# Attention, then a Fourier mix and a feed-forward layer, on one core: transform parts moved behind the next scores, and one row's copies made once and brought in by DMA

## The chip, the core and the metric

The kernel runs on one core of a Trainium2 chip. The core has a matrix engine (PE; its weight loads are shown apart as PEld), a vector engine (DVE), an activation engine (ACT), a general engine (POOL) and a queue engine (SP) that issues most of the transfers. Each engine takes its own instructions in order and waits on semaphores for the others. The metric is the device time of one execution in microseconds.

## What is computed

Attention over 4 batches, 8 heads, 768 tokens of head size 64: each token sees the 4 first tokens and the 128 up to itself. Its output, with heads side by side, is `x` of 4 x 768 x 512. Then a two-dimensional Fourier transform of each batch is added, and a normalized feed-forward layer on top:

```python
keep = is_sink | in_window
scores = np.where(keep, scale * q @ k.T, -1e9)
x = softmax(scores) @ v
u = x + real(fft(fft(x, axis=1), axis=2))
un = (u - mean(u)) / sqrt(var(u) + 1e-6)
out = u + relu(un @ w_ch1) @ w_ch2
```

## The kernel before

**Attention** runs in 96 steps. A step `s` is block `g = s // 4` of 128 query tokens (24 blocks, six to a batch) and a pair of heads `k = s % 4`. The work on one pair is spread over later steps by a table of lags: scores on PE at once (`scores`), a merge and a masked maximum on DVE one step later (`merge`, `soft1`), the exponential on ACT after two (`expo`), the transposes of a pair of pairs after three (`trans_p`, PE), copies and masks on ACT and POOL, and attention times values after seven (`av`, PE). Per block come a transpose of the sink columns (`trans_sink`, seven steps after the block's first, PE, tile `pk`), the turn back to tokens (`turn_x`, tile `x`) and the scaled store into `u` (`store_x`, DVE). Because the lags of `trans_p`, `av` and `turn_x` fall on even steps, an odd step gives PE nothing but its scores, `trans_sink` (where `k` is 3) and transform work.

A step issues its loads on SP first, then the scores, then what the lists in `SCHEDULE` name for ACT, DVE, POOL and PE, in their order. From step 97 on (`CUT`) the order on an engine is left to the scheduler of the framework. The scores have two PSUM buffers of two banks each, so the scores of step `s + 1` need `soft1` of step `s - 1` to be done.

**The transform** of batch b is created when its fourth block is stored (steps 25, 49, 73 and 97) and put into the same steps as events. First the blocks are folded (`fold_n`, `fold_m`, on DVE and POOL; `fold_hi` on ACT, `fold_lo` on DVE): tiles `f`, `gh`, `gl`. Fifteen steps after its creation `stage1` starts: five products `za0`, `za1`, `zr`, `zb0`, `zb1`, each in two parts, one for a step; then `stage2a` and `stage2b` (`dc`, `a`, `b`). Each result lies in one PSUM bank, is copied by ACT (`z_hi`, `a_copy`) and finished by DVE (`z_lo`, `combine`), and then the next product takes a bank: tag `fft`, or for a product begun at a step with `k` of 2 (`X_AT`) the bank `x`, which `turn_x` uses too.

**The first token's row.** Token 0 has no place in the six blocks. Its attention output for all batches is made on DVE in steps 10 to 20 and stored into `x0_dram` (`first_row`). Per batch, `load_row` brings it in on 33 partitions (tile `xr`), `put_row` copies it to row 0 of block 3 of `u` once the folds have read that row, `mid_sum` folds it, `mid_hi` copies it rounded into `sph` and `mid_row` puts what the rounding left into partition 32 of `sph`. The last matmul of `za0`, `za1` and `zr` reads `sph`. All of these are DVE's, except that in the last batch `mid_hi` is ACT's; `ROW` holds their steps after the creation.

**The feed-forward layer** begins on PE when attention ends and runs alone from about 283 us on.

Of the kernel before, what the change touches and what calls it, by code (L numbers as in the profile page):

```python
# [11 lines left out]
F32 = mybir.dt.float32  # L12
F32R = mybir.dt.float32r
# [3 lines left out]
ALU = mybir.AluOpType  # L17
PSUM = bass.MemoryType.PSUM

P = 128  # L20
# [41 lines left out]
FILL_AT, FILL = (24, 36), 0  # L62
FOLD_AT, FOLD_LAST, FOLD_ENG = (0, 4, 8), (0, 4, 8), "VG"

F_N, F_M, F_S, ROW = (3, 3), (4, 5), (6, 7), (5, 8, 10)
EV_A = 0

SINK0_AT = 3, 3, "V"
PHASE = 36

STEP_LAG = {"merge": 1, "soft1": 1, "expo": 2, "sink_p": 2, "trans_p": 3, "copy_p": 4, "newer_p": 5, "older_p": 5, "av": 7}
BLOCK_AT = {
    "copy_x": 11,
# [138 lines left out]
def kernel(  # L212
# [17 lines left out]
    def f32(ap):  # L230
        return ap.bitcast(F32)
# [7 lines left out]

    w_dram = [dpool.tile([P, 2, len(LEFT) * 2 * P], F32, name=f"w2s{q}") for q in range(NF // 2)]  # L240
    x0_dram = dpool.tile([B * H, D], F32, name="x0d")


    prm = cpool.tile([P, 2, 2], I32, name="prm")
# [22 lines left out]
    def run(general):  # L267
        tag = "g" if general else ""
        with ExitStack() as p1:
# [8 lines left out]
            def at(s, eng, fn):  # L278
                ev.setdefault((s, eng), []).append(fn)

            def run_ev(s, eng):
                for fn in ev.pop((s, eng), ()):
                    fn()
# [36 lines left out]
            def bank(b, name):  # L320
# [5 lines left out]
                pool, t, n = banks[turn[0] % len(banks)]  # L326
                return pool.tile([P, 512], F32, tag=t, name=f"{name}_{b}", bufs=n)

            def fourier(b, at, ready):
                u = uview(b)  # L330
                gh = npool.tile([P, NHALF, DM], F32R, tag="gh", name=f"gh_{b}", bufs=1)
# [7 lines left out]
                    return t_[name]  # L339

                def load_row():
                    t_["x0"] = fw.tile([NR, DM], F32, tag="xr", name=f"xr_{b}")
                    nc.sync.dma_start(t_["x0"], x0_dram[H * b:H * b + H].rearrange("(o h) d -> o (h d)", o=1).broadcast_to([NR, DM]))

                def fold_n(eng, j, odd):
                    t = fw.tile([P, DM], F32, tag=f"f{odd}", name=f"f{odd}_{b}_{j}", bufs=2 - odd)
# [16 lines left out]
                def fold_lo(j):  # L363
                    V.tensor_tensor(gl[:, j], t_.pop(("g", j)), f32(gh[:, j]), op=ALU.subtract)  # L364

                def mid_sum():
                    r = t_["x0"]
                    V.tensor_tensor(r[:, 1:256], r[:, 1:256], r[:, 511:256:-1], op=ALU.add)

                def mid_hi():  # L370
                    (A.copy if b == B - 1 else V.tensor_copy)(sph[:NR, :257], t_["x0"][:, :257])

                def mid_row():
                    t = t_["x0"]
                    lo = sph[NR - 1:NR, :257]
                    V.tensor_tensor(lo, t[NR - 1:NR, :257], f32(lo), op=ALU.subtract)

                def put_row():
                    V.tensor_copy(u[NHALF][0:1], t_["x0"][0:1])

                def stage1(kind, mc, part, parts):
                    ps = t_[f"z{kind}{mc}"] if part else psum(f"z{kind}{mc}")
# [77 lines left out]
                        nc.sync.dma_start(u_dram[b][:, blk, :], t)  # L460

                tail = b == B - 1 or general
                at(1, "S", load_row)
                for j in range(NHALF):
                    k = ready[j]
                    e0, e1 = FOLD_TAIL if tail else FOLD_ENG
# [4 lines left out]
                    at(k + F_M[1], e1, lambda j=j: fold_m(eng[e1], j, 1))  # L471
                    at(k + F_S[0], "A", lambda j=j: fold_hi(j))
                    at(k + F_S[1], "V", lambda j=j: fold_lo(j))
                at(ready[0] + ROW[0], "V", put_row)
                at(ready[0] + ROW[1], "V", mid_sum)
                at(ready[0] + ROW[2], "A" if b == B - 1 else "V", mid_hi)
                at(ready[0] + ROW[2], "V", mid_row)
                k = ready[2] + S1
                n1, na, nb = PARTS_TAIL if tail else PARTS[b]
                for i, (kind, mc) in enumerate((("a", 0), ("a", 1), ("r", 0), ("b", 0), ("b", 1))):  # L480
# [173 lines left out]
            def window_attention(fourier, load_constants):  # L654
                with ExitStack() as pa:
# [166 lines left out]
                        T.matmul(flat, st.pop(("skt", g)), st["vs", g // NB], start=False, stop=True, skip_group_check=True)  # L822

                    def trans_sink(g):
                        ps = ps_t.tile([P, P], F32R, tag="pt", name=f"pk_{g}")
                        T.transpose(ps, st.pop(("sk", g)).rearrange("p g h s -> p (g h s)"), ident_r)
                        st["pk", g] = ps

# [15 lines left out]
                    with ExitStack() as man:  # L844
# [116 lines left out]
                        at(15, "A", first_exp)  # L961
                        for i in range(NS):
                            at(17 + i, "V", lambda i=i: first_row(i))

                        table = {
                            "merge": merge, "soft1": soft1, "expo": expo, "sink_p": sink_p, "trans_p": trans_p, "copy_p": copy_p,
# [1 line left out]
                            "trans_sink": trans_sink, "turn_x": turn_x, "inverse": inverse, "store_x": store_x,  # L968
                            "sink_hi": lambda g: g and g % NB == 0 and sink_hi(g // NB), "sink_lo": lambda g: g and g % NB == 0 and sink_lo(g // NB),
                        }  # L970
                        s = 0
                        extra.append(lambda name: ps_t.tile([P, 512], F32, tag="x", name=name)
                                     if s % NP in X_AT and not X_NOT[0] <= s <= X_NOT[1] and s < len(steps) - 2 else None)
                        while s < last:
                            g, k = divmod(s, NP)
                            if s == CUT:
                                man.close()
                            if s == len(steps) + 1:
                                pb.close()
                                start_ffn(s)  # L980
                            wraps = g < NQ and g % NB > 0 and kb(g) % NSLOT == 0
                            if k == 0 and not wraps:
                                load_qk(g + 2)
                            elif k == 1 and g % NB == 0 and g < NQ:
                                load_k(kb(g + 2) + 1)
                            elif k == 2 and g % NB == 4 and g + 2 < NQ:
                                load_sink(g // NB + 1)
                            elif k == 3 and g < NQ:
                                load_v(kb(g))
                                if g % NB == 2:  # L990
                                    load_v(kb(g) + 1)
                            run_ev(s, "S")
                            lag(scores, s, 0)
                            if k == 3 and wraps:
                                load_qk(g + 2)
                            if s == 0:
                                a, b, e = SINK0_AT
                                at(a, "A", lambda: sink_hi(0))
                                at(b, e, lambda: sink_lo(0))
                            for e in "AVGT":  # L1000
                                for op in SCHEDULE[s >= PHASE][e][k]:
                                    if op in EVENTS:
                                        if (s, op) == (4, "G"):
                                            load_constants()
                                        run_ev(s, op)
                                    elif op in STEP_LAG:
                                        lag(table[op], s, STEP_LAG[op])
                                    else:
                                        at_ = s - BLOCK_AT[op]
                                        if at_ % NP == 0 and 0 <= at_ // NP < NQ:  # L1010
                                            table[op](at_ // NP)
                                            if op == "store_x" and at_ // NP % NB == 3:
                                                b = at_ // NP // NB
                                                fourier(b, lambda d, e, f, s=s: at(s + d, e, f), FOLD_AT if b < B - 1 else FOLD_LAST)
                            s += 1
# [3 lines left out]
            def general_attention(fourier):  # L1019
                for b in range(B):  # L1020
                    u = uview(b)
                    with ExitStack() as pa:
# [70 lines left out]
                        V.tensor_copy(u[NHALF][0:1], u[0][0:1])  # L1093
                        nc.sync.dma_start(x0_dram[H * b:H * b + H].rearrange("(o h) d -> o (h d)", o=1), x0)
                    ev = []
                    fourier(b, lambda d, e, f: ev.append((d, ENGINES.index(e), len(ev), f)), FOLD_AT)
                    for it in sorted(ev, key=lambda t: t[:3]):
                        it[3]()
# [503 lines left out]
```

## Time and profile before

| | before |
|---|---|
| median of 3 runs | 768.49 us (767.43 to 771.24) |
| the profiled execution | 768.74 us |
| its span, first to last instruction | 767.0 us |
| busy, share of the span | PE 97%, PEld 82%, DVE 78%, ACT 45%, POOL 24% |
| mean granted clock of PE | 0.995 |
| mean DMA rate | 169 GB/s |

A row of a time line has the start and the length in us, the engine, the line of the program, the operation, the written and read tiles, the shape and the count of merged instructions; in brackets stands how long the engine had been idle and what ended that. PE's matmuls are pipelined and their ends are modelled, so a start is surer than a length. A granted clock of 0.5 is half speed. The whole program is profiled once, so a single row is one execution's.

### The profile page before, as it was taken

The page shows a single profiled execution, that of the slowest core. Times are in us where ns is not written, and L with a number is a line of the kernel's source. Part 1 is how long each engine was busy: PE and PEld are TensorE (multiplying, and loading weights), DVE is VectorE, ACT ScalarE, POOL GpSimd, SP SyncE. Part 2 cuts the span into 40 slices and gives each one's busy share as a digit, 9 for nine tenths or more (in the row PEclk, how much of TensorE's full clock was granted, in tenths as well). Part 3 has the DMA queues.
Part 4 walks back from the last instruction along what each step waited for, and adds up shares of the span by engine and source line. Part 5 has one row for each costly group of instructions (what it writes and reads, how often), then busy time and mean ns, then how long its engine had stood idle before and what let it go on. Part 6 is the DMA issues. An engine that isn't in the chain of part 4 may idle for free.

```text
span 767.0 us, 14157 instructions
## 1 busy us (share of the span) xinstructions
PE 742.3 (97%) x4903; PEld 626.7 (82%) x4903; DVE 600.6 (78%) x1641; ACT 345.9 (45%) x896; POOL 181.6 (24%) x286
## 2 busy tenths in 40 slices
PE   7999998998999999999999999999999999999996
PEld 5666775766788778788989899899899998998995
DVE  6878588799799989969877978778895888764435
ACT  4877666666643223444545333333333333333330
POOL 2557267467574445400000000000000000000001
PEclk9999999999999999999999999999999999999998
DMA  9845514532313446323546757755577557556661
GB/s 294 277 112 165 144 56 151 160 104 94 111 56 138 138 165 219 110 110 141 190 151 247 227 160 231 230 171 191 170 226 235 173 172 243 160 176 188 208 193 60
DMA packets 95008, 129.40 MB, mean 169 GB/s; under 512 B 5932, under 2 KB 60844, under 8 KB 94544
## 3 DMA queue, kind: packets, MB, share of 16 engines
q1 hardware_dynamic: 94352, 124.26, 51.1%
q0 software_dynamic: 288, 3.76, 1.3%
q8 instruction: 41, 0.67, 0.4%
q10 hardware_dynamic: 288, 0.39, 0.1%
q14 instruction: 39, 0.32, 0.1%
HBM read 104.26 MB, written 24.13 MB: 167 GB/s over the span
## 4 chain that ended last, share of the span: by engine, by line
PE 78%; DVE 16%; issue 2%; ACT 1%; POOL 1%; DMA 1%; SPq 0%; DVEq 0%; ACTq 0%; POOLq 0%
PE h L638 31%; PE p L1313 25%; PE xt L808 5%; PE s L721 5%; PE o L1139 3%; PE pt L770 2%; PE za L393 2%; PE zb L393 1%; DVE f L348 1%; PE x L820 1%; DVE sm L739 1%; DVE gl L364 1%; PE zr L393 1%; DVE w2r L602 1%; DMA vt<-in_v_sink_dram 1%
## 5 line engine op out<-in xcount | busy, mean ns | idle before, releaser
L1313 PE MATMUL p<-w_ring,h_sums 128*128 128x256 f32 x936 | 131.3, 283 | 0.1
L1313 PEld LDWEIGHTS p<-w_ring,h_sums 128*128 128x128 f32 x936 | 122.9, 191 | 3.6 <-DVE u L1143 0.3
L1261 ACT CAST h_sums<-sums 128x256 fp32r<-128x256 f32 (+2 forms) x158 | 89.7, 568 | 70.5 <-PE p L1313 28.6
L1262 DVE TENSOR_TENSOR h_sums<-sums,h_sums 128x256 fp32r<-128x256 f32 (+2 forms) x158 | 98.3, 622 | 17.5 <-ACT h_sums L1261 16.5
L1313 PE MATMUL p<-w2t,h_sums 128*128 128x256 f32 x702 | 110.3, 283 | 0.0
L1335 POOL TENSOR_TENSOR u<-u,u 128x512 f32<-128x512 f32 x3 | 3.8, 1293 | 422.9 <-DVE u L1335 422.9
L1313 PEld LDWEIGHTS p<-w2t,h_sums 128*128 128x128 f32 x702 | 97.9, 191 | 3.1
L638 PE MATMUL h<-un_slots,w 128*128 128x512 f32 x396 | 96.5, 392 | 0.0
L638 PE MATMUL h<-un_last,w 128*128 128x512 f32 x396 | 96.4, 392 | 0.0
L638 PEld LDWEIGHTS h<-un_slots,w 128*128 128x128 f32 x396 | 72.7, 188 | 14.0
L638 PEld LDWEIGHTS h<-un_last,w 128*128 128x128 f32 x396 | 72.3, 188 | 14.4 <-DVE un_slots L553 0.7
L745 ACT ACTIVATE sm<-sm,mx 128x132 f32<-128x132 f32 x192 | 75.8, 399 | 14.4 <-DVE mx L739 14.4
L1475 ACT ACTIVATE sums<-h 128x512 f32<-128x512 f32 x40 | 23.9, 597 | 96.8 <-PE h L638 96.8
L721 PE MATMUL s<-ring,q 64*128 64x260 f32 x320 | 55.6, 430 | 7.2 <-DVE mx L739 7.2
L1163 DVE STREAM_TRANSPOSE unf<-un 32x128 f32<-32x128 f32 x192 | 58.1, 302 | 2.8
L1272 DVE TENSOR_TENSOR sums<-sums 128x256 f32<-128x256 f32 x39 | 16.4, 422 | 47.6 <-ACT sums L1475 47.3
L1443 ACT ACTIVATE sums<-h 128x512 f32<-128x512 f32 x40 | 23.9, 599 | 64.8 <-PE h L638 64.8
L739 DVE CUSTOM_DVE_ANT_0 sm<-s,mask 128x132 f32<-128x132 f32 x192 | 47.5, 285 | 4.5 <-PE s L719 2.4
L727 DVE COPY_PREDICATED s<-older,s 128x256 f32<-128x256 uint8 x80 | 33.8, 422 | 16.9 <-PE s L721 16.6
L721 PEld LDWEIGHTS s<-ring,q 64*128 64x128 f32 x320 | 25.0, 186 | 21.3 <-issue 10.0
L808 PE MATMUL xt<-ptl,ldv 128*64 128x128 f32 x384 | 39.8, 288 | 0.0
L745 ACT ACTIVATION_READ_ACCUMULATOR sm<-sm,mx 128x1 f32 x192 | 36.7, 191 | 0.0
(239 smaller groups left out, 1378.1 us busy)
## 6 DMA issues: line engine op xcount, KB each, us to landing
w_ring<-w2s SPq DMA_DIRECT2D x62, 512.0 KB, 4.3
w2t<-w2s SPq DMA_DIRECT2D x93, 256.0 KB, 3.2
raw<-in_moe_w_ch_dram SPq DMA_DIRECT2D x32, 512.0 KB, 3.3
w2s<-w_ring SPq DMA_DIRECT2D x16, 512.0 KB, 3.0
ldv<-in_v_dram SPq DMA_DIRECT2D x28, 256.0 KB, 2.8
ring<-in_qk_dram SPq DMA_DIRECT2D x24, 264.0 KB, 4.3
w2s<-w2t SPq DMA_DIRECT2D x24, 256.0 KB, 3.1
out_dram<-u SPq DMA_DIRECT2D x22, 256.0 KB, 4.6
```

What stands on the lines that cost most here:

```text
L393: T.matmul(ps[:, :NK], a, c, start=i == 0, stop=i == len(mm) - 1)
L638: T.matmul(ps[:, :tb], a[:, cs], x[:, :, cc, :], start=n == 0, stop=n == 3 * NCC - 1)
L721: T.matmul(ps[:, j, :P + W], st["q", g][rows, hp, :], keys(g, 2 * hp + j), start=True, stop=True)
L727: V.copy_predicated(ps[:, :, P + NS:P + W], older[qi > 2], ps[:, :, 0:P])
L739: V.tensor_tensor_reduce(sm[:, h % 4], ps[:, j, P:P + W], mask[min(qi, 3)], -SCALE, 3.0e38, ALU.add, ALU.min, accum_out=mx[:, 0, h:h + 1])
L745: A.activation(sm[:, h % 4], sm[:, h % 4], AF.Exp, bias=mx[:, 0, h:h + 1], scale=-1.0, accum_out=mx[:, 1, h:h + 1])
L808: T.matmul(ps[D * j:D * j + D, p, :], st["v", kb(g) - i][:, h, :], a[:, h % 4, :], start=i == 0, stop=i == n - 1)
L1163: V.transpose(unf[32 * q:32 * q + 32, :, r], un[r].rearrange("p (c q j) -> p c q j", c=NCC, q=4)[:, :, q])
L1261: A.copy(hc_hi[:, left(a, n)], src)
L1262: V.tensor_tensor(hc_lo[:, left(a, n)], src, f32(hc_hi[:, left(a, n)]), op=ALU.subtract)
L1313: T.matmul(acc[i][:, 2 * P * tp:2 * P * tp + 2 * P], x, w, start=q == 0 and tp == 0 and n == 0, stop=q == end and n == 2, skip_group_check ...
L1443: A.activation(r4[:, 0].rearrange("p t w -> p (t w)"), ps, AF.Relu)
```

## The change

Two things are changed.

**1. Held parts.** In odd steps from 9 to 96, the transform parts and `trans_sink` are not issued in their step but kept in a list, and issued right after the scores of the next step. Nothing else of a step is held; a held part issues PE instructions alone. The bank that a part takes is still chosen by the step it belonged to (`at_s`). For steps below 36, `trans_sink` takes the bank `fft` instead of the bank `pt`, which `trans_p` uses.

**2. The row.** A new function `middle_rows` folds the rows of all four batches at once and splits them into a rounded and a remaining part (tiles `xr`, `xm`, 4 partitions), at steps 24 to 29, and stores both into a new buffer `xm_dram`. Per batch, `load_row` is now a transfer of two rows from there into partitions 0 and 32 of `sph`, nine steps after the transform's creation, and `put_row` a transfer of `x0_dram` into block 3 of `u`, five steps after it. `mid_sum`, `mid_hi` and `mid_row` are gone.

```diff
-F_N, F_M, F_S, ROW = (3, 3), (4, 5), (6, 7), (5, 8, 10)
+F_N, F_M, F_S, ROW = (3, 3), (4, 5), (6, 7), (9, 5)
+ROW_AT = 24, 26, 27, 28, 29
+HOLD = 9, 97
...
+            def middle_rows(b, n, at):
+                x = fw.tile([B, DM], F32, tag="xr", name=f"xr_{b}")
+                xm = fw.tile([B, 2, DM // 2 + 1], F32R, tag="xm", name=f"xm_{b}")
+                def load():
+                    nc.sync.dma_start(x[:n], x0_dram[H * b:H * (b + n)].rearrange("(o h) d -> o (h d)", o=n))
+                def fold():
+                    V.tensor_tensor(x[:n, 1:256], x[:n, 1:256], x[:n, 511:256:-1], op=ALU.add)
+                def hi():
+                    A.copy(xm[:n, 0], x[:n, :257])
+                def lo():
+                    V.tensor_tensor(xm[:n, 1], x[:n, :257], f32(xm[:n, 0]), op=ALU.subtract)
+                def store():
+                    nc.sync.dma_start(xm_dram[b:b + n], f32(xm[:n]))
+                for s, e, fn in zip(ROW_AT, "SVAVS", (load, fold, hi, lo, store)):
+                    at(s, e, fn)
...
                 def load_row():
-                    t_["x0"] = fw.tile([NR, DM], F32, tag="xr", name=f"xr_{b}")
-                    nc.sync.dma_start(t_["x0"], x0_dram[H * b:H * b + H].rearrange("(o h) d -> o (h d)", o=1).broadcast_to([NR, DM]))
+                    nc.sync.dma_start(f32(sph[:NR:NR - 1, :257]), xm_dram[b])
...
-                def mid_sum():
-                    r = t_["x0"]
-                    V.tensor_tensor(r[:, 1:256], r[:, 1:256], r[:, 511:256:-1], op=ALU.add)
-
-                def mid_hi():
-                    (A.copy if b == B - 1 else V.tensor_copy)(sph[:NR, :257], t_["x0"][:, :257])
-
-                def mid_row():
-                    t = t_["x0"]
-                    lo = sph[NR - 1:NR, :257]
-                    V.tensor_tensor(lo, t[NR - 1:NR, :257], f32(lo), op=ALU.subtract)
-
                 def put_row():
-                    V.tensor_copy(u[NHALF][0:1], t_["x0"][0:1])
+                    nc.sync.dma_start(u[NHALF][0:1], x0_dram[H * b:H * b + H].rearrange("(o h) d -> o (h d)", o=1))
...
-                at(1, "S", load_row)
+                at(ROW[0], "S", load_row)
...
-                at(ready[0] + ROW[0], "V", put_row)
-                at(ready[0] + ROW[1], "V", mid_sum)
-                at(ready[0] + ROW[2], "A" if b == B - 1 else "V", mid_hi)
-                at(ready[0] + ROW[2], "V", mid_row)
+                at(ready[0] + ROW[1], "S", put_row)
...
                     def trans_sink(g):
-                        ps = ps_t.tile([P, P], F32R, tag="pt", name=f"pk_{g}")
+                        pool, tag = (ps_fft, "fft") if NP * g + BLOCK_AT["trans_sink"] < PHASE else (ps_t, "pt")
+                        ps = pool.tile([P, P], F32R, tag=tag, name=f"pk_{g}")
...
+                        def run_held(step):
+                            nonlocal at_s
+                            at_s = step
+                            run_ev(step, "T")
...
                             lag(scores, s, 0)
...
+                            held, hold = hold, []
+                            for fn in held:
+                                fn()
+                            at_s = s
...
                                 for op in SCHEDULE[s >= PHASE][e][k]:
-                                    if op in EVENTS:
+                                    if e == "T" and k % 2 and HOLD[0] <= s < HOLD[1]:
+                                        if op == "T":
+                                            hold.append(lambda s=s: run_held(s))
+                                        elif op == "trans_sink" and k == BLOCK_AT[op] % NP:
+                                            hold.append(lambda g=(s - BLOCK_AT[op]) // NP: 0 <= g < NQ and trans_sink(g))
+                                    elif op in EVENTS:
```

What that does to the order on the engines, at three places. In a name such as `s_11_2_1320`, `s` is the tile of the scores, 11 the block, 2 the pair of heads, and the last number the buffer's; line numbers differ between the two programs.

PE in the middle of batch 0's transform (steps 45 and 46; `zr0` is a product of `stage1`, `xt` attention times values), before:

```order
L721 MATMUL s_11_1_1300<-ring_87,q_11_1021 128x260 x2
L393 MATMUL zr0_0_1288<-cst_94,gl_0_763 128x386
L393 MATMUL zr0_0_1288<-cst_94,gh_0_762 128x386 x2
L393 MATMUL zr0_0_1288<-cst_94,gl_0_763 128x386
L393 MATMUL zr0_0_1288<-cst_row_95,sph_96 128x386
L721 MATMUL s_11_2_1320<-ring_87,q_11_1021 128x260 x2
L808 MATMUL xt_9_1274<-ptl_9_3_1271,ldv_11_1109 64x128 x2
```

And of the change:

```order
L731 MATMUL s_11_1_1304<-ring_88,q_11_1023 128x260 x2
L731 MATMUL s_11_2_1319<-ring_88,q_11_1023 128x260 x2
L406 MATMUL zr0_0_1292<-cst_95,gl_0_767 128x386
L406 MATMUL zr0_0_1292<-cst_95,gh_0_766 128x386 x2
L406 MATMUL zr0_0_1292<-cst_95,gl_0_767 128x386
L406 MATMUL zr0_0_1292<-cst_row_96,sph_97 128x386
L818 MATMUL xt_9_1278<-ptl_9_3_1275,ldv_11_1113 64x128 x2
```

The scores of the even step moved from behind the second part of `zr` to the place ahead of it, so two steps' scores stand in a row, and the part now stands directly ahead of attention times values.

PE before the transforms begin (steps 19 and 20; `pt` are the transposes of `trans_p`, `pk` that of the sink columns), before:

```order
L770 MATMUL pt_3_3_584<-ident_63,sm_3_2_499 128x128 x4
L721 MATMUL s_4_3_591<-ring_87,q_4_321 128x260 x2
L826 MATMUL pk_3_610<-ident_r_111,sk_3_502 128x128
L721 MATMUL s_5_0_615<-ring_87,q_5_407 128x260 x2
L808 MATMUL xt_3_630<-ptl_3_1_573,ldv_4_484 64x128 x2
```

And of the change:

```order
L780 MATMUL pt_3_3_587<-ident_63,sm_3_2_502 128x128 x4
L731 MATMUL s_4_3_594<-ring_88,q_4_324 128x260 x2
L731 MATMUL s_5_0_616<-ring_88,q_5_408 128x260 x2
L837 MATMUL pk_3_619<-ident_r_112,sk_3_505 128x128
L818 MATMUL xt_3_633<-ptl_3_1_576,ldv_4_487 64x128 x2
```

The sink transpose moved behind the next step's scores.

DVE while batch 1 is folded (steps 59 and 60; `ISA` rows are `soft1` with its tile of scores, `mx` its read of the maximum), before:

```order
L739 ISA sm_14_2_1766,mx_14_1707<-s_14_2_1722,mask2_133 128x132
L739 ISA mx_14_1707 128x1
L371 CAST sph_96<-xr_1_1449 33x257
L376 TENSOR_TENSOR sph_96<-xr_1_1449,sph_96 1x257
L727 COPY_PREDICATED s_14_3_1750<-older0_129,s_14_3_1750 128x2x128
L739 ISA sm_14_2_1766,mx_14_1707<-s_14_3_1750,mask2_133 128x132
```

And of the change:

```order
L749 ISA sm_14_2_1768,mx_14_1708<-s_14_2_1717,mask2_134 128x132
L749 ISA mx_14_1708 128x1
L737 COPY_PREDICATED s_14_3_1752<-older0_130,s_14_3_1752 128x2x128
L749 ISA sm_14_2_1768,mx_14_1708<-s_14_3_1752,mask2_134 128x132
L749 ISA mx_14_1708 128x1
```

The two instructions on `sph` are gone from between one step's softmax and the next step's merge, and so are `put_row` and `mid_sum` earlier in the same batch. On SP, in the place of one load of `xr` for each batch, there stand for batch 1 a transfer into `us_1_3` between the loads of key block and value tile 15, and one into `sph` behind that tile. After step 97 the scheduler's order on PE differs in one place: the second half of batch 3's `za0` stands ahead of the first product `o0`.

More of the change, by code (lines that the diff above doesn't have):

```diff
@@ L241 @@
     x0_dram = dpool.tile([B * H, D], F32, name="x0d")
+    xm_dram = dpool.tile([B, 2, DM // 2 + 1], F32, name="xmd")
     prm = cpool.tile([P, 2, 2], I32, name="prm")
@@ L963, in window_attention @@
                             at(17 + i, "V", lambda i=i: first_row(i))
+                        middle_rows(0, B, at)
                         table = {
@@ L970, in window_attention @@
                         }
-                        s = 0
+                        s = at_s = 0
                         extra.append(lambda name: ps_t.tile([P, 512], F32, tag="x", name=name)
-                                     if s % NP in X_AT and not X_NOT[0] <= s <= X_NOT[1] and s < len(steps) - 2 else None)
+                                     if at_s % NP in X_AT and not X_NOT[0] <= at_s <= X_NOT[1] and at_s < len(steps) - 2 else None)
+                        hold = []
+                        def run_held(step):
+                            nonlocal at_s
+                            at_s = step
+                            run_ev(step, "T")
                         while s < last:
@@ L1095, in general_attention @@
                     ev = []
+                    middle_rows(b, 1, lambda s, e, fn: fn())
                     fourier(b, lambda d, e, f: ev.append((d, ENGINES.index(e), len(ev), f)), FOLD_AT)
```

## The prediction

> **What bounds the kernel now.** I first read the busy time of each engine in stretches cut where the character of the work changes. The columns are the length, then busy time and instructions of PE, PEld, DVE, ACT and POOL, the granted clock, the DMA share and GB/s.
>
> ```profile
> 15.00:55.00 40.00, 38.45 (x363) 26.77 (x363) 31.76 (x161) 31.54 (x129) 22.43 (x50) 1.00 0.69 226
> 55.00:70.50 15.50, 13.17 (x112) 8.30 (x112) 14.19 (x61) 12.36 (x48) 11.11 (x19) 1.00 0.47 124
> 70.50:110.00 39.50, 39.39 (x330) 30.22 (x330) 24.48 (x104) 25.12 (x91) 18.92 (x40) 1.00 0.42 123
> 110.00:128.50 18.50, 15.82 (x123) 10.65 (x121) 16.19 (x59) 11.27 (x44) 16.52 (x27) 0.91 0.26 60
> 128.50:157.00 28.50, 28.47 (x235) 21.69 (x236) 21.70 (x93) 18.32 (x67) 11.74 (x26) 1.00 0.58 180
> 157.00:188.00 31.00, 27.66 (x231) 19.65 (x233) 28.20 (x99) 19.36 (x71) 22.73 (x37) 1.00 0.37 113
> 188.00:208.00 20.00, 20.00 (x163) 15.29 (x163) 15.40 (x59) 11.98 (x45) 10.54 (x20) 1.00 0.35 120
> 208.00:283.00 75.00, 71.88 (x412) 60.40 (x413) 73.21 (x133) 26.83 (x60) 39.28 (x36) 1.00 0.35 118
> 283.00:767.00 484.00, 475.96 (x2876) 424.73 (x2874) 366.83 (x833) 183.12 (x330) 24.58 (x19) 0.99 0.57 183
> ```
>
> Three kinds of stretch alternate. Where the transform runs (70.5 to 110, 128.5 to 157, 188 to 208) PE is filled to the last tenth and DVE has a quarter or more free: **PE-dense** stretches. Where a batch's blocks are folded (55 to 70.5, 110 to 128.5, 157 to 188) DVE is busy for 88 to 92% and PE stands idle for 2.33, 2.68 and 3.34 us: **fold** stretches, bound by DVE. From 208 to 283 both are nearly full. The last 484 us, the feed-forward part, hold none of the changed lines and I leave them as they are. So the change can be worth PE's idle time of the fold stretches, a lost clock (below), and whatever PE's own sequence costs in the dense ones.
>
> The chain that ended last, followed from 117.8 us, shows who holds PE in a fold stretch:
>
> ```profile
> 117.82 0.69 DVE sph L371
> ...
> 118.53 0.74 DVE sph L376
> ```
>
> The row's copy and its low part (`mid_hi`, `mid_row`) stand on the chain. PE's next scores had to wait for the softmax behind them, and then the clock was halved:
>
> ```profile
> 123.95 1.24 PE L721 MATMUL s<-ring,q 64*128 64x260 f32 x4 [2.40 <-DVE mx L739]
> ```
>
> ```profile
> 123.80:127.20 3.40, 3.25 (x21) 2.29 (x22) 2.51 (x14) 1.66 (x9) 3.17 (x9) 0.50 0.00 0
> ```
>
> **The change, part by part: the row.** These are the busy times of all instructions on tile `xr` (after the length: DVE, then ACT), in the stretches where DVE is the bound or nearly so:
>
> ```profile
> 55.00:70.50 15.50, 2.19 (x3) 0.00 (x0) 1.00 0.47 124
> 110.00:128.50 18.50, 1.90 (x3) 0.00 (x0) 0.91 0.26 60
> 157.00:188.00 31.00, 3.01 (x4) 0.00 (x0) 1.00 0.37 113
> 208.00:283.00 75.00, 2.03 (x3) 0.40 (x1) 1.00 0.35 118
> ```
>
> All of it goes. In the first fold stretch 2.19 us of DVE stand against 2.33 of idle PE: I take 2.0. In the second, 1.90 against the wait of 2.40: I take 1.9. With that wait down to half a microsecond I expect the clock not to drop; 3.25 us of matmuls at half rate would have taken 1.6 us less, so 1.6. In the third, 3.01 against 3.34, but held transform parts come later there (below): I take 2.3. After 208 the row's 2.03 us leave a DVE that is 98% busy, while PE idles only 3.12 us in 75, and the order from step 97 on is the scheduler's, which now puts the second half of the first `za` ahead of the first `o` matmuls: I take 0.7, with bounds of -1.0 and +2.0.
>
> How sure is the size of a removed instruction? Its time is not always its own:
>
> ```profile
> L368 DVE TENSOR_TENSOR xr<-xr x4: 404/436/1486, 58.4 to 219.2; 33x255 f32<-33x255 f32 x4
> L371 DVE CAST sph<-xr x3: 282/757/1408, 62.8 to 176.5; 33x257 fp32r<-33x257 f32 x3
> L376 DVE TENSOR_TENSOR sph<-xr,sph x4: 418/735/777, 63.1 to 225.6; 1x257 fp32r<-1x257 f32 x4
> ```
>
> ```profile
> 176.53 1.27 POOL L348 TENSOR_TENSOR f<-u 128x512 f32<-128x512 f32 x1
> ```
>
> ```profile
> 176.54 1.41 DVE L371 CAST sph<-xr 33x257 fp32r<-33x257 f32 x1
> ```
>
> The cast of 0.28 us took 1.41 when it began with a POOL fold of 1.27. If that wait only passes to the next DVE instruction, a batch gives 0.40 + 0.28 + 0.42 = 1.1 us, and the three fold terms fall from 6.2 to 3.3. I stay near the full size, because what follows the cast is a softmax that reads its scores from PSUM, and by the time DVE comes to its next instruction on SBUF alone the fold has run. [...]
>
> What is added: one sum and one difference on DVE for all batches and one copy on ACT, at steps 26 to 28, in the stretch from 15 to 55. No row shows 4 partitions; by the shortest rows above 0.40 + 0.42, between 0 and 2.3 (the longest). DVE has 8 us free there, so nothing; if that cover were gone, 0.8. The new DMAs are SP's. `put_row` is now a transfer, and SP, which issues in order, must wait for the folds that read row 0 of block 3, POOL's above all:
>
> ```profile
> 50.80 1.46 POOL L348 TENSOR_TENSOR f<-u 128x512 f32<-128x512 f32 x1
> ```
>
> ```profile
> ring<-in_qk_dram SPq DMA_DIRECT2D x24, 264.0 KB, 4.3
> ```
>
> Behind it stand value tile 8 and query block 9, which PE first reads at step 36; the transfer is written at step 30. Six steps of about 1.74 us (below: 31.3 us from step 19 to step 37) are 10 us for a load of 4.3: nothing, and 1 for 1 once it comes more than 6 us late. The load of `sph` stands six steps ahead of the first matmul that could read it.
>
> **The held parts.** PE's rows show what a change of partner costs (s are the scores, pk the sink transpose, zr a transform part, xt attention times values):
>
> ```profile
> 35.38 0.71 PE L721 MATMUL s<-ring,q 64*128 64x260 f32 x4
> 36.27 0.25 PE L826 MATMUL pk<-ident_r,sk 128*128 128x128 f32 x1 [0.18 <-ACT pta L777]
> 36.45 0.71 PE L721 MATMUL s<-ring,q 64*128 64x260 f32 x4
> 37.09 0.44 PE L808 MATMUL xt<-ptl,ldv 128*64 128x128 f32 x4
> ...
> 66.71 1.15 PE L721 MATMUL s<-ring,q 64*128 64x260 f32 x8
> 67.79 0.44 PE L808 MATMUL xt<-ptl,ldv 128*64 128x128 f32 x4
> ...
> 143.00 0.71 PE L721 MATMUL s<-ring,q 64*128 64x260 f32 x4
> 143.64 0.45 PE L393 MATMUL zr<-cst,gl 128*128 128x386 f32 x1
> ...
> 144.46 0.34 PE L393 MATMUL zr<-cst_row,sph 128*128 128x386 f32 x1
> 144.73 0.71 PE L721 MATMUL s<-ring,q 64*128 64x260 f32 x4
> 145.37 0.44 PE L808 MATMUL xt<-ptl,ldv 128*64 128x128 f32 x4
> ```
>
> One step's scores followed by anything else take 0.64 us (143.00 to 143.64, 144.73 to 145.37); two in a row take 1.08 (66.71 to 67.79). Today an odd step pays 0.64, then 0.27 from the part's last matmul to the scores, then 0.64: 1.55 beside the part itself. With the scores together it is 1.08, or 1.18 where the second score still pays the 0.10 that 0.64 lies above half of 1.08, and again about 0.27 at the part's end: 0.10 to 0.20 less. Held parts of the transform stand in 24 steps, 17 of them in dense stretches (8, 5 and 4): 17 x 0.15 = 2.6, bounds 1.7 and 3.4. Against it: the scores now come up to 1 us earlier and may find the softmax before last unfinished, with the filler behind them; I take off 0.5, at most 1.7.
>
> For pk the sequence takes 1.71 us (35.38 to 37.09), of which part is a wait for ACT to empty the bank that pk shares; with a bank of its own and behind both scores it is 1.08 + 0.18 = 1.26, or 1.36 if the second score pays the dearer change. So 0.35 to 0.45 in each of steps 11 to 27; I take 0.3 x 5 = 1.5, bounds 0 and 2.2.
>
> **Sum**: 1.5 + 2.6 - 0.5 + 2.0 + 1.9 + 1.6 + 2.3 + 0.7 = 12.1 us, from the profiled execution's 768.74 (span 767.0; the median of the runs is 768.49): **756.6**. With every bound on the bad side 0 + 1.7 - 1.7 + 1.1 + 1.1 + 0 + 1.1 - 1.0 = 2.3, so 766.4; on the good side 2.2 + 3.4 + 2.2 + 2.4 + 1.6 + 3.0 + 2.0 = 16.8, so 751.9.
>
> **Rivals.** (A) *The clock drops all the same*, there or at another place: 1.6 us back, 758.2. For it: fold stretches keep some idle PE. Against it: the other stalls, shorter than 2.40, had no drop. [...] The trace has the drop at the end of that stall.
> (B) *The waits for POOL move on* to other DVE instructions: 2.9 back, 759.5.
> (C) *The held parts do not do what they are for*: the scores wait for DVE as long as the switch had cost, 2.6 lost and 1.2 more of waits: 760.4. For it speaks the third fold stretch, where DVE already waits for a part's result:
>
> ```profile
> 174.76 0.42 DVE L446 TENSOR_TENSOR d<-asb,b 128x257 f32<-128x257 f32 x1 [1.03 <-PE b L441]
> ```
>
> (D) *DVE becomes the bound of the dense stretches too, and the kernel is slower.* A held part ends one score later, so its eviction (ACT, then DVE in order) keeps DVE 0.64 us longer, and the softmax and the next scores queue behind. If all 24 held steps lost 0.64, 15.4 us, against 10.0 of the other terms: 774. It decides where DVE has under 0.64 us free per pair of steps. It has 15.0 us over 8 pairs, 6.8 over 6 and 4.6 over 4, so 1.9, 1.1 and 1.2; only 157 to 188, with 2.8 over 7, is past that point.
> (E) A, B and C at once: 764.9.
>
> **Chances**: forecast 0.50, A 0.12, B 0.15, C 0.10, E 0.08, D 0.05. The range from 752 to 765 leaves out D, half of E and the ends. A measurement here tells about 0.5% from no change: A to C are faster by more than that, E lies on the edge. Faster 0.87, same 0.08, slower 0.05.
>
> **What would show it.** Right: no instruction on `xr` after 55 us; PE's wait near 122 under 1 us and no stage at half clock after the first microseconds; in dense stretches 1.1 us for two scores in a row, and pk behind them without a wait for ACT. Wrong: waits of scores for `mx` in front of held parts, DVE waits for `za`, `zb` or `b` well over the present 0.6 to 1.0, longer `gl` and `f` in place of the row's, or loads of q and values that PE waits for.

## The result, and the profile after

The changed kernel takes **760.88 us** (median of 4 runs, 760.06 to 762.22) against 768.28 before (4 runs): a ratio of 0.9898, 95% interval 0.9877 to 0.9919, so 7.4 us less. I had forecast 756.6, 12.1 less. The direction and the range held; the gain is six tenths of the forecast.

To compare runs stretch by stretch I cut them at the start of the second softmax instruction of a step (`soft1`; steps 13, 39, 55, 75, 89 and 95). These are the windows of before, with the columns of the prediction's first table:

```profile
27.48:71.16 43.68, 40.19 (x379) 27.74 (x375) 36.40 (x167) 33.95 (x132) 27.11 (x54) 1.00 0.52 147
71.16:109.97 38.81, 38.81 (x328) 29.75 (x325) 23.82 (x103) 24.74 (x91) 18.31 (x38) 1.00 0.41 121
109.97:157.23 47.26, 44.55 (x359) 32.60 (x358) 38.14 (x154) 29.82 (x110) 28.30 (x53) 0.96 0.46 133
157.23:193.21 35.98, 32.64 (x272) 23.48 (x270) 33.19 (x115) 22.50 (x84) 27.64 (x44) 1.00 0.36 111
193.21:209.14 15.93, 15.93 (x132) 12.19 (x130) 11.29 (x46) 9.78 (x33) 6.60 (x15) 1.00 0.35 117
```

and the same steps after:

```profile
27.17:68.33 41.16, 39.51 (x381) 28.12 (x378) 34.47 (x167) 33.96 (x133) 26.53 (x54) 1.00 0.52 153
68.33:105.75 37.42, 37.24 (x325) 29.92 (x324) 23.38 (x100) 24.27 (x91) 18.15 (x38) 1.00 0.42 125
105.75:150.25 44.50, 42.39 (x361) 31.96 (x359) 36.69 (x149) 29.76 (x110) 27.57 (x53) 1.00 0.46 139
150.25:185.94 35.69, 32.45 (x286) 24.58 (x284) 31.55 (x111) 22.91 (x84) 27.20 (x44) 1.00 0.36 112
185.94:201.10 15.16, 14.94 (x120) 11.66 (x118) 11.51 (x46) 9.53 (x32) 6.70 (x14) 1.00 0.39 123
```

The first stretch holds the sink transposes of steps 15 to 35 and the first fold, the second is the first dense one, the third holds the second fold and the second dense part, the fourth the third fold, the fifth the last dense part. They give 2.5, 1.4, 2.8, **0.3** and 0.8 us. The clock of the third is back at 1.00. The fourth is the odd one: DVE lost 1.64 us of work there, PE next to none of its idle time (3.34 before, 3.24 after).

The cuts are DVE's, and the last two windows do not hold the same work of PE: the fourth has 286 matmuls after against 272, the fifth 120 against 132. The second softmax instruction of step 89 stands 2.12 us behind the start of its scores before, and 2.88 after. PE's own rows, the scores of steps 89 and 95, before and after:

```profile
191.09 0.71 PE L721 MATMUL s<-ring,q 64*128 64x260 f32 x4
207.28 0.71 PE L721 MATMUL s<-ring,q 64*128 64x260 f32 x4
```

```profile
183.06 1.15 PE L731 MATMUL s<-ring,q 64*128 64x260 f32 x8
199.24 0.71 PE L731 MATMUL s<-ring,q 64*128 64x260 f32 x4
```

Cut at the scores of the same steps, the fourth stretch takes 33.61 us against 34.62, and the fifth 16.18 against 16.19. So the third fold gave 1.0 us and the last dense part nothing. In the other stretches the two cuts agree within 0.1 us on what was gained.

PE's time line after, in that fourth stretch, shows why it did not give more:

```profile
162.09 0.71 PE L731 MATMUL s<-ring,q 64*128 64x260 f32 x4
164.82 0.71 PE L731 MATMUL s<-ring,q 64*128 64x260 f32 x4 [2.01 <-DVE mx L749]
165.46 0.51 PE L433 MATMUL a<-cst,za 128*128 128x258 f32 x2
165.80 0.28 PE L433 MATMUL a<-cst_row,zr 128*128 128x258 f32 x1
...
169.92 0.71 PE L731 MATMUL s<-ring,q 64*128 64x260 f32 x4 [0.86 <-DVE mx L749]
170.56 0.74 PE L433 MATMUL a<-cst,za 128*128 128x258 f32 x4
...
175.01 0.71 PE L731 MATMUL s<-ring,q 64*128 64x260 f32 x4 [0.36 <-DVE mx L749]
175.65 0.98 PE L454 MATMUL b<-cst,zb 128*128 128x258 f32 x6
```

Each wait has a held part (`a`, `a`, `b`) standing behind it that needs nothing from the softmax awaited. In the old order PE ran that part first, and the wait was shorter by it. In a dense stretch the two scores now stand together as meant, 1.08 us in a row:

```profile
81.45 1.15 PE L731 MATMUL s<-ring,q 64*128 64x260 f32 x8
82.53 0.44 PE L406 MATMUL zr<-cst,gl 128*128 128x386 f32 x1
```

### The profile page after: what moved, and what is told of

Its sections match the earlier page's. It is cut to its first block, busy times and chain, and to the rows that moved or that the text cites. A ratio compares the mean times of both kernels' runs of the same rounds, so it can differ in the third digit from the quotient of the medians.

```text
span 758.7 us, 14154 instructions
## 1 busy us (share of the span) xinstructions
PE 735.8 (97%) x4903; PEld 627.1 (83%) x4903; DVE 594.5 (78%) x1628; ACT 345.0 (45%) x896; POOL 180.0 (24%) x286
## 4 chain that ended last, share of the span: by engine, by line
## 5 line engine op out<-in xcount | busy, mean ns | idle before, releaser
L731 PE MATMUL s<-ring,q 64*128 64x260 f32 x320 | 50.4, 415 | 8.3 <-DVE mx L749 7.3
```

Of the source, the lines that this page charges most:

```text
L731: T.matmul(ps[:, j, :P + W], st["q", g][rows, hp, :], keys(g, 2 * hp + j), start=True, stop=True)
```

## The experiments

The theory after the result, **H**: a held part gains about 0.17 us where PE is full, and costs where the next scores wait for DVE. The rival, **W**: the third fold gained nothing because DVE's waits for POOL moved to other instructions, and the held parts cost nothing. The table has the length of each stretch in each run's profile (us, cut at the softmax of the same steps), for the last two also the length cut at PE's scores of these steps (columns PE), and the median of its runs. Each ratio is to runs of before made together with that kernel's (medians 768.05 to 768.68).

| | 13-39 | 39-55 | 55-75 | 75-89 | 89-95 | 95-end | 75-89, PE | 89-95, PE | median | ratio, 95% |
|---|---|---|---|---|---|---|---|---|---|---|
| before | 43.68 | 38.81 | 47.26 | 35.98 | 15.93 | 557.88 | 34.62 | 16.19 | 768.28 | |
| changed | 41.16 | 37.42 | 44.50 | 35.69 | 15.16 | 557.57 | 33.61 | 16.18 | 760.88 | 0.9898 (0.9877-0.9919) |
| held parts alone | 41.93 | 37.44 | 47.80 | 38.92 | 15.16 | 557.91 | 36.86 | 16.17 | 768.52 | 0.9997 (0.9981-1.0013) |
| row alone | 42.91 | 38.82 | 44.41 | 33.73 | 15.93 | 559.01 | 32.37 | 16.18 | 763.26 | 0.9920 (0.9895-0.9944) |
| row, sink transposes held | 41.14 | 38.84 | 44.43 | 33.90 | 15.81 | 557.69 | 32.26 | 16.34 | 761.12 | 0.9892 (0.9869-0.9916) |
| 77 to 87 free | 41.14 | 37.41 | 44.53 | 33.71 | 15.57 | 557.60 | 32.12 | 16.10 | 759.52 | 0.9871 (0.9846-0.9896) |
| 57, 65, 81, 83, 85 free | 41.15 | 37.42 | 43.92 | 33.97 | 15.56 | 557.85 | 32.38 | 16.10 | 759.70 | 0.9876 (0.9856-0.9897) |
| 57, 65, 77 to 87 free | 41.14 | 37.42 | 43.92 | 33.72 | 15.57 | 559.27 | 32.12 | 16.11 | 759.22 | 0.9879 (0.9855-0.9904) |
| row and bank | 41.97 | 38.82 | 44.46 | 33.71 | 15.94 | 557.79 | 32.36 | 16.19 | 761.76 | 0.9919 (0.9887-0.9950) |
| row, held in the old bank | 41.13 | 38.84 | 44.43 | 33.86 | 15.84 | 557.61 | 32.25 | 16.34 | 760.71 | 0.9910 (0.9877-0.9943) |

Up to step 95, stretches that hold the same instructions in the same order agree within 0.05 us from profile to profile. So a difference of 0.2 us in a stretch can be read, where a whole time could not tell it. Between 75 and 95 only the PE columns tell what PE's order is worth.

**Held parts alone.** The changed kernel with the row made per batch as before; of the edit, the lines that put its operations back in their old places:

```diff
-                at(ready[0] + ROW[1], "S", put_row)
+                at(ready[0] + ROW[0], "V", put_row)
+                at(ready[0] + ROW[1], "V", mid_sum)
+                at(ready[0] + ROW[2], "A" if b == B - 1 else "V", mid_hi)
+                at(ready[0] + ROW[2], "V", mid_row)
```

> Only the held parts and sink transposes are in; the row is made per batch as before. Theory H (the held parts gain in the dense stretches and lose in the third fold stretch, where PE used to run them while it waited for a softmax): sink transposes 1.0, dense stretches 2.4 less, third fold stretch 1.7 more, so 766.6 us; from softmax step 75 to 89 it takes 1 to 2 us longer than the 35.98 us of before. Theory W (the third stretch gained nothing because the waits for POOL moved on, and the held parts cost nothing there): 764.9 us, and 35.98 us stay within 0.4. Both: the 2.40 us wait at step 60 and the half-speed stage behind it stay, since the row's cast is back.

By themselves the held parts gain nothing, where H had 766.6 us in all: what they win before step 55 (1.75 and 1.37) they lose between 55 and 89 (0.54, and 2.24 by PE's scores, 2.94 by DVE's softmax). The wait at step 60 came back with 2.17 us and its half-speed stage (clock 0.50 from 123.17 to 126.58 us), as expected. In the third fold they lost more than H had, and there a wait of 2.77 us for `mx` was followed by half the clock a second time:

```profile
167.54:170.96 3.42, 1.07 (x7) 0.72 (x7) 3.39 (x10) 0.89 (x4) 2.39 (x3) 1.00 0.65 216
170.96:174.37 3.41, 3.41 (x20) 2.89 (x19) 0.71 (x5) 1.62 (x6) 1.74 (x4) 0.50 0.00 0
```

**Row alone.** Nothing held, sink transposes in their old bank.

```diff
-HOLD = 9, 97
+HOLD = 0, 0
...
-                        ps = pool.tile([P, P], F32R, tag=tag, name=f"pk_{g}")
+                        ps = ps_t.tile([P, P], F32R, tag="pt", name=f"pk_{g}")
```

> Only the row's change is in; transform parts and sink transposes stand where they stood before, in the old bank. Theory H: first fold stretch 1.2 less, second 2.2 with the clock's drop gone, third (softmax step 75 to 89, 35.98 us before, 35.69 with both changes) 2 less, so 34.0 us there and 762.9 us in all. Theory W: the third stretch stays at 35.7 to 36, and 764.9 us in all.

33.73 us and 763.26: H, and W falls. The row by itself is worth 2.25 us in the third fold by either cut, as forecast, and 2.85 in the stretch of the second; from 13 to 39 it gives 0.77, where H had 1.2.

**The third fold's parts free again**, and **no transform part held** (`HOLD_NOT` is `range(9, 97)` there):

```diff
+HOLD_NOT = 77, 79, 81, 83, 85, 87
...
-                                        if op == "T":
+                                        if op == "T" and s in HOLD_NOT:
+                                            run_ev(s, op)
+                                        elif op == "T":
                                             hold.append(lambda s=s: run_held(s))
```

> The changed kernel, but the transform parts of steps 77 to 87 are issued in their own step again; all else as in the changed kernel. Theory H: the waits of the scores of 2.01 and 0.86 us at 164.8 and 169.9 us shrink by the parts that fill them again, step 75 to 89 falls from 35.69 to about 34.0 us, in all 759.2 us. Theory W: no change, 760.9 us within 0.4.

> The changed kernel without any held transform part: row, held sink transposes and their own bank. Theory H: the dense stretches lose the 2.4 us that holding gave (softmax steps 39 to 55, 37.42 us, become 38.6), the third fold stretch gains 1.7, so 761.6 us. Theory W: dense stretches lose 2.4, the third gains nothing, 763.3 us.

The third fold takes 33.71 and 33.90 us, and by PE's scores 32.12 and 32.26 against 33.61, so holding cost 1.3 to 1.5 us of PE's time there. The rest of the 1.8 to 2.0 us that the softmax shows is the late softmax of step 89, and comes back in the next column. The whole takes 759.52 and 761.12 us, near H's 759.2 and 761.6 and not W's 760.9 and 763.3. PE's time line of the kernel with 77 to 87 free, at the same place as above: the part stands ahead of the scores again, and of the wait of 2.01 us are left 0.34.

```profile
163.68 0.71 PE L732 MATMUL s<-ring,q 64*128 64x260 f32 x4
164.32 0.50 PE L434 MATMUL a<-cst,za 128*128 128x258 f32 x2
164.66 0.28 PE L434 MATMUL a<-cst_row,zr 128*128 128x258 f32 x1
165.29 0.71 PE L732 MATMUL s<-ring,q 64*128 64x260 f32 x4 [0.34 <-DVE mx L750]
```

That is more than the part's own 0.8 us; in the first kernel of the next experiment, where 81 is free and 77 and 79 are held, the same wait is 1.47 us, which suggests that their parts count in it too. Against the kernel without any held transform part, the changed one wins 1.42 us in the first dense stretch and 0.16 (by PE's scores) in the last, loses 1.35 in the third fold, and is even from 55 to 75 (44.43 and 44.50).

**The five waiting steps free**, and **both selections**:

Two more kernels with other steps in `HOLD_NOT`; the first is the one that later expectations call the kernel that holds only where PE is full.

> The changed kernel, but transform parts are issued in their own step at 57, 65, 81, 83 and 85, the five odd steps where the next scores waited 0.29 to 2.01 us for a softmax with the part behind them; the other held parts stay. Theory H (a held part costs where the next scores wait for DVE, and gains 0.17 us elsewhere): softmax steps 55 to 75 fall from 44.50 to about 43.6 us, 75 to 89 stand at 33.7 and 89 to 95 at 15.2, in all 758.0 us. Rival: holding pays only from 39 to 55 and the rest of the second batch's parts gain nothing, so 55 to 75 stays at 44.4, in all 758.9 us.

> The changed kernel, but transform parts are issued in their own step at 57 and 65 and at all odd steps from 77 to 87. If the savings of the two earlier selections add (softmax steps 55 to 75: 43.92 us with 57 and 65 free, against 44.50; 75 to 89: 33.71 us with 77 to 87 free, against 35.69), 55 to 75 takes 43.9 us, 75 to 89 33.7 and 89 to 95 15.6, and the whole 758.8 us, a span of 756.5 to 757.2. Rival: the parts of the second batch's end shift the third stretch, and one of the two savings is lost, 759.4 us.

With 57 and 65 free, 55 to 75 takes 0.58 us less than in the changed kernel and 0.51 less than with nothing held: the other parts of the second batch do gain, and the rival that they gain nothing falls. The savings of the two selections add in their stretches, and yet the totals (759.5, 759.7, 759.2) cannot be told apart: the first kernel missed its 758.0 us, and the second lies between its 758.8 and the rival's 759.4. From 89 to 95 both take 15.6 us by the softmax, not the 15.2 that the first expectation had, and 16.1 by PE's scores, where the changed kernel has 16.2: freeing the third fold's parts lets the softmax of step 89 come earlier. The first has a half-speed stage at the start in its profile (clock 0.50 from 14.19 to 17.61 us). In the second the end from step 95 took 559.27 us in place of 557.6 to 557.9, as it had with the row alone. This is one place of that, in the kernel with both selections:

```profile
222.34 1.28 POOL L638 TENSOR_TENSOR w<-cv,w 128x512 fp32r<-128x512 f32 x1 [3.80 <-issue]
222.41 1.76 DVE L612 SCALAR_TENSOR_TENSOR w2r<-raw,w2r 128x512 int32<-128x512 int32 x1
```

and with 77 to 87 free:

```profile
223.31 1.91 POOL L638 TENSOR_TENSOR w<-cv,w 128x512 fp32r<-128x512 f32 x1 [3.80 <-issue]
223.39 0.68 DVE L612 SCALAR_TENSOR_TENSOR w2r<-raw,w2r 128x512 int32<-128x512 int32 x1
```

The same two instructions, POOL's row 0.07 and 0.08 us ahead; in the one DVE is held up (1.76 us against 0.68), in the other POOL (1.91 against 1.28). There are a few such meetings after step 95. Where they fell to DVE's cost, PE waited 0.5 us more for `d` and 0.8 more for `zb` (1.60 against 0.81), with the order of its work unchanged.

**The sink transposes: bank or place?** Nothing held but the new bank kept (`HOLD = 0, 0`), and held but in the old bank:

> The row's change, and the bank of its own for the sink transposes before step 36, but nothing is held. With the row alone softmax steps 13 to 39 take 42.91 us, with held sink transposes in the new bank 41.15. Theory (the bank does it, by ending the waits of 0.18 to 0.88 us for ACT's copy; the place gives the rest): 41.3 to 41.9 us. Rival (the place does it, since behind both scores ACT has long been done): 42.6 to 42.9 us.

> The row's change, and sink transposes behind the next step's scores but in the old bank; no transform part is held. Theory of the bank: the waits for ACT's copy stay in part, 41.9 to 42.6 us from softmax step 13 to 39. Rival (the place does it): 41.1 to 41.4 us.

From 42.91 the bank alone takes 0.94, the place alone 1.78, both together 1.77. The 41.97 us of the bank alone lie outside what either side had expected of it; the 41.13 of the place alone are the rival's. So the place is enough, the bank by itself gives half, and on top of the place it adds nothing. A wait for ACT stays in the old bank, but it stands behind both scores now and is paid once from step 13 to 39:

```profile
59.41 1.38 PE L732 MATMUL s<-ring,q 64*128 64x260 f32 x8
61.22 0.25 PE L837 MATMUL pk<-ident_r,sk 128*128 128x128 f32 x1 [0.43 <-ACT pta L788]
```

**The row's new work on POOL.** In the changed kernel the row's own instructions are these (count, then shortest, median and longest in ns):

```profile
L341 DVE TENSOR_TENSOR xr<-xr x1: 733/733/733, 45.6 to 45.6; 4x255 f32<-4x255 f32 x1
L344 ACT CAST xm<-xr x1: 407/407/407, 46.4 to 46.4; 4x257 fp32r<-4x257 f32 x1
L347 DVE TENSOR_TENSOR xm<-xr,xm x1: 409/409/409, 47.5 to 47.5; 4x257 fp32r<-4x257 f32 x1
```

None stands after 55 us, and the new ones take DVE 1.14 us. With the row alone, steps 13 to 30 were 0.37 us longer than before (28.09 against 27.72): I had priced this at nothing. Moved to POOL:

```diff
-                    V.tensor_tensor(x[:n, 1:256], x[:n, 1:256], x[:n, 511:256:-1], op=ALU.add)
+                    G.tensor_tensor(x[:n, 1:256], x[:n, 1:256], x[:n, 511:256:-1], op=ALU.add)
...
-                for s, e, fn in zip(ROW_AT, "SVAVS", (load, fold, hi, lo, store)):
+                for s, e, fn in zip(ROW_AT, "SGAGS", (load, fold, hi, lo, store)):
```

> As the kernel that holds only where PE is full, with the one fold and the one low part of all batches' rows on POOL in place of DVE. Theory: the 0.3 us that the row made once costs from softmax step 13 to 30 (26.44 us with it, 26.16 with the old row) are DVE's, through the 0.48 us wait of scores for a softmax at 46.9 us, and this wait goes: 26.15 us there. Rival: the wait comes from elsewhere (ACT's copy, or DVE waiting for POOL's instructions), and 26.4 stays or grows.

From 13 to 30 the theory holds: the softmax wait of 0.48 us went, and these steps took 25.46 us against 26.46. But PE now waited 0.73 us for POOL's `pta` at 52.6, steps 30 to 39 took 16.05 us against 14.69, and so 13 to 39 took 41.51 against 41.15 on DVE. The whole was 759.59 (0.9887, 0.9866 to 0.9907). The row's sums are in the way on either engine.

**POOL's folds in halves:**

```diff
-                    eng.tensor_tensor(t, u[j], u[NHALF + j], op=ALU.subtract if odd else ALU.add)
+                    for h in (slice(0, 256), slice(256, DM)) if eng is G else (slice(0, DM),):
+                        eng.tensor_tensor(t[:, h], u[j][:, h], u[NHALF + j][:, h], op=ALU.subtract if odd else ALU.add)
```

> As the kernel that holds only where PE is full, with each of POOL's folds between blocks as two instructions of 128x256 in place of one of 128x512. Theory P (a DVE instruction on SBUF waits until the POOL instruction has ended): no DVE instruction waits longer than about 0.7 us, the difference f of 1.76 us at 115.6 falls under 1.3, and the three fold stretches are 0.3 to 1.0 us shorter in all. Rival (POOL and DVE share the memory's time and not whole instructions, or the sum of the waits stays the same): no change within 0.2, or longer by what two more instruction starts cost POOL.

On the mechanism this told nothing: in the kernel that it was built on, the `f` of 1.76 us had become 1.12 without any halving, and DVE's longest instruction between 50 and 190 us went from 1.23 to 1.21. On the time the rival holds: steps 55 to 75 took 44.15 us against 43.92, and POOL's instructions on `f` 21.7 us in all against 19.8. The whole was 760.46 (0.9897, 0.9878 to 0.9917), with a half-speed stage in the third fold, of which below.

**A longer wait.** Two additions on DVE whose results nobody reads, ahead of the softmax behind the wait of 2.01 us:

```diff
                 for s, e, fn in zip(ROW_AT, "SVAVS", (load, fold, hi, lo, store)):
                     at(s, e, fn)
+                if n > 1:
+                    at(81, "V", fold)
+                    at(81, "V", fold)
```

> The changed kernel with two more DVE additions of 4x255 at step 81, whose results nobody reads, right ahead of the softmax for which PE waits 2.01 us. Theory C (the clock drops behind a PE wait of more than about 2.1 us, whatever DVE does in it): the wait grows to 2.4 to 2.8 us and a stage of 3.4 us at clock 0.50 follows within about 1.2 us of its end; from softmax step 75 to 89 it takes the wait's growth and 1.5 more, 37.6 to 38.2 us against 35.69. Rival (the drop needs something else, such as the row's cast): the growth alone, 36.1 to 36.5 us, and no half-speed stage.

The two took 0.84 and 0.73 us, so the wait grew to 3.11. Half the clock followed for 3.41 us, and the stretch took 38.16 us: 1.10 by the wait and the other 1.37 with the clock. The whole was 763.22 (0.9928, 0.9910 to 0.9946). The row's cast is not needed for the drop. That the wait's length decides it, as theory C has it, does not follow: with POOL's folds in halves, half the clock came behind a window of 3.41 us in which PE stood idle for 1.58 us.

## Why the prediction was right, and where it was off

- **Sink transposes**: forecast 1.5; measured 1.75 (before to held alone) and 1.77 (row alone to row with transposes held) from step 13 on. Ahead of that the one of step 11 costs 0.15: from its scores to those of step 13, 4.12 us against 3.97. Two reasons were named, a bank of its own and the place behind both scores, and the place is the one that counts. That the size fits is partly luck: the sum has five transposes, steps 11 to 27, and the gain comes from six, steps 15 to 35.
- **Row, first fold**: forecast 2.0; measured 0.77, of which the new sums take back 0.37. The cover was mis-sized. I set the row's 2.19 us of DVE against all of PE's 2.33 us of idle time, but part of that idle time were the sink transposes' own waits for ACT, in PE's time line of before:

```profile
56.16 0.25 PE L826 MATMUL pk<-ident_r,sk 128*128 128x128 f32 x1 [0.61 <-ACT pta L777]
60.48 0.71 PE L721 MATMUL s<-ring,q 64*128 64x260 f32 x4 [0.94 <-DVE mx L739]
63.61 0.25 PE L826 MATMUL pk<-ident_r,sk 128*128 128x128 f32 x1 [0.61 <-ACT pta L777]
```

  Only the 0.94 us was DVE's to give, and the row alone removed it.
- **Row, second fold, and the clock**: forecast 1.9 + 1.6; measured 2.85 together. The half-speed stage went as said (rival A fell; that the later wait of 2.01 us kept full clock may be owed to where it lay, below). Split by PE's time in that stretch, with the same matmuls, 1.46 us are busy time, which is the half-speed stage's (44.55 to 43.09), and 1.39 are idle time (2.71 to 1.32).
- **Row, third fold**: forecast 2.3; measured 2.25. Rival B, that the waits for POOL only move on, holds for single instructions and not for this sum. One of them, in the second fold of the changed kernel; an `f` of that size took 0.69 us in the kernel before at 180.85 us, with no fold of POOL's beside it, and here it ends 0.56 us behind POOL's:

```profile
115.11 1.70 POOL L373 TENSOR_TENSOR f<-us,us 128x512 f32<-128x512 f32 x1
...
115.61 1.76 DVE L373 TENSOR_TENSOR f<-us,us 128x512 f32<-128x512 f32 x1
```

- **Held parts, dense stretches**: forecast 0.15 us a part, 2.6 in all; measured 1.37 to 1.42 for the 8 parts of the first, 0.17 to 0.18 each, and about 0.5 for the second batch's outside of 57 and 65. In the last stretch PE's scores show 0.02 to 0.16; the 0.65 to 0.77 of the softmax cuts are for the most part the late softmax of step 89. So 1.9 to 2.1 in all. Rival D, that DVE becomes the bound and the dense stretches grow, falls: none did.
- **Held parts, fold stretches**: this is **the step that failed**. "Against it: the scores now come up to 1 us earlier and may find the softmax before last unfinished, with the filler behind them; I take off 0.5, at most 1.7." The runs show 1.3 to 1.5 us in the third fold by PE's scores, and 0.6 from 55 to 75, which freeing 57 and 65 gave back and which is the whole gain of the second batch's other parts: some 2 us in place of 0.5, more than the bound. I had the mechanism, and priced it as one allowance over all steps. The stretches where it counts were those in which PE's idle time was DVE's already. Rival C named the third fold and its wait for `b`, and its 760.4 us lies close, but it let the dense stretches gain nothing, and they did gain. Net, the held transform parts gain the 0.3 us by which the changed kernel's stretches differ from those without them, where I had 2.1. This and the first fold's row are 3.0 of the 3.8 us that the profile's gain of 8.3 is short of the forecast.
- **After step 95**: forecast 0.7; measured 0.3. Between the row alone (559.01) and the row with sink transposes held (557.69) the end moves by 1.3 us with the same order of PE's work there, so the term was not the row's to forecast, and its coming near is luck.

The remaining 0.3 us of the profile's 8.3 lies before step 13: PE's scores of step 5 begin 0.57 us earlier (13.32 against 13.89), where nothing was changed, and from there to the softmax of step 13 the change loses the rest.

## What to carry to other kernels

An instruction that waits for nothing is worth most where its engine would otherwise wait: moving it behind the next waiting instruction pays only where the engine is full, so such a rule wants a list of steps and not one range. Before setting work removed on one engine against idle time of another, go through the idle time's releasers one by one, since several owners can share it. Stretches cut at the same step of each run show gains and losses to some hundredths of a microsecond that cancel in the total. Cut them on the engine whose time is asked for: a cut on another engine moves with that engine's lag, here by 0.8 us at step 89.

## What the runs showed of the hardware

**Half the clock and idle PE.** In the clock records of the traces of before and of the changed kernel, every change of the granted clock lies at a whole multiple of 3.413 us from the record's start: at 34, 35 and 221 times that in before, at 219 times in the changed kernel. The windows here are cut on that grid. In the changed kernel the wait of 2.01 us fell across a boundary, 1.36 us idle on one side and 0.66 on the other, with full clock kept:

```profile
160.74:164.16 3.42, 2.06 (x16) 1.41 (x14) 3.42 (x6) 1.53 (x7) 2.98 (x6) 1.00 0.59 187
164.16:167.57 3.41, 2.75 (x23) 2.10 (x24) 2.40 (x12) 2.28 (x10) 1.54 (x3) 1.00 0.50 154
167.57:170.98 3.41, 2.55 (x19) 1.63 (x18) 2.83 (x14) 1.82 (x4) 3.33 (x6) 1.00 0.22 77
```

POOL's folds in halves, where PE stood idle for 1.58 us inside one window:

```profile
162.74:166.15 3.41, 1.83 (x18) 1.11 (x17) 3.38 (x14) 1.43 (x6) 2.51 (x4) 1.00 0.73 235
166.15:169.56 3.41, 3.41 (x18) 2.80 (x15) 1.66 (x9) 1.75 (x7) 1.76 (x5) 0.50 0.02 6
```

Six windows inside the work were followed by half the clock: with 1.58 us of idle PE in this one, 1.83 with the longer wait, 1.91 with 57, 65, 81, 83 and 85 free, 2.17 and 2.35 with the held parts alone, and 2.27 in before. Full clock was kept behind 1.65 us in before (11.19 to 14.60 us) and behind about 1.8 with 77 to 87 free (10.31 to 13.73 us), so the idle time in this profile does not settle it alone. The longer wait lost 1.37 us with the clock, the wait of 2.01 us none. That its place on the grid made the difference is an estimate from these windows; no run moved a wait and kept its length.

**POOL and DVE.** In the rows after step 95, one of the two took its own time and the other much more: DVE's 1.08 us more in the one kernel (1.76 against 0.68), POOL's 0.63 in the other (1.91 against 1.28). The starts of the rows do not tell who that will be: POOL's lay 0.07 and 0.08 us ahead, and it went through in one case only. PE's waits behind two such meetings differ by 1.3 us between these two runs.

**A small addition beside POOL.** The addition on 4 partitions and 255 columns took 0.73 us on DVE in the changed kernel and 0.73 to 0.84 in the three of the longer wait's, where the one on 33 partitions and as many columns had taken 0.40 at best. The partitions are not what tells them apart: the subtraction on 4 partitions and 257 columns took 0.41. The one of the changed kernel had a POOL masking instruction beside it (from 45.00 to 46.09 us, the addition at 45.63), and the 33-partition ones of 0.40 and 0.41 us in the kernel before (at 219.17 and 113.61 us) met none. No run moved that POOL instruction away.
